# P transposed by row halves of the array into two PSUM banks, in one group with the next scores

## The chip, the core and the metric

The program runs on one core of a Trainium2 chip. The core has five engines that work side by side, each in the order of its own queue: TensorE (PE in the profile, with its weight loads as PEld), VectorE (DVE), ScalarE (ACT), GpSimd (POOL) and SyncE (SP), which issues transfers here. TensorE writes to PSUM, a memory of eight banks of 2 KB for each of 128 partitions; ScalarE and VectorE copy from there to SBUF. The metric is the device time of one execution in microseconds. All times below are in microseconds unless marked ns.

## What is computed

```python
# q, k, v: (8, 8, 576, 64) = (batch, heads, sequence, head size)
scores = scale * np.matmul(q, k.transpose(0, 1, 3, 2))
kth = np.partition(scores, -32, axis=-1)[..., -32:-31]
scores = np.where(scores >= kth, scores, -1e9)
attn = np.exp(scores - np.max(scores, axis=-1, keepdims=True))
attn = attn / (np.sum(attn, axis=-1, keepdims=True) + 1e-09)
x = np.matmul(attn, v)            # then (batch * sequence, heads * head size) = (4608, 512)
h = x @ w_in                      # (512, 2048)
g = 0.5 * h * (1.0 + erf(h / sqrt(2)))
out = g @ w_out                   # (2048, 512)
```

Attention that keeps the 32 largest scores of each row is followed by a two-layer perceptron with an exact gelu. Everything is 32-bit floating point on the chip; the two weight matrices arrive as 64-bit numbers and are converted there.

## The kernel before

**Items.** The attention is cut into 144 items. A main item is a pair of heads of one batch and 128 of the first 512 query rows; its tile `s` holds 2 x 576 scores for each of 128 rows. 576 keys are four blocks of 128 and a rest of 64, so the last 64 keys of both heads stand side by side in the middle of `s`. A last item (16 of 144, two per batch) takes the last 64 query rows of two pairs of heads.

**One item goes through the engines like this.** TensorE computes scores: `s_ps` for the 512 first keys (two banks, one for each head; each matmul uses 64 rows of the array, one half for each head) and `t_ps` for the last keys. ScalarE copies both to `s`. VectorE finds the 32nd largest of each row (`top_k`: four MAX8 and three MATCH_REPLACE8 for each head). GpSimd makes two small bias values of it (`threshold`). ScalarE runs `softmax` in two halves, one for each head: a Prelu that throws what is below the 32nd far down, and an Exp that also sums the row. GpSimd adds a small number to the sums (`add_small`, tile `den`), VectorE takes the reciprocal (`inverse`, tile `rden`) at the end of the next item's `top_k`, and GpSimd multiplies both heads' rows by it (`normalise`, in place in `s`). TensorE transposes the result P in blocks, ScalarE copies the transposed blocks to `pt` (or `ptt` for last items), and TensorE multiplies them with V (`attend`, tile `o`), for two main items at a time, so in every second iteration, and for each last item. ScalarE copies `o` to `xT`, from which the perceptron reads.

**The order is written out by hand.** The loop from line 659 emits every engine's queue. In iteration n it emits: scores of item n+2; attend of item n-3, if it completes a pair; the first half of softmax(n-1); up to eight pieces of the perceptron, spread between the others (`mlp`, 2 instructions of `y_ps` with 512 columns or 4 of `h_ps` with 256 columns each); the transposes of item n-2 in three pieces (the last keys' `tails`, then `main(0)` and `main(1)`, one for each head, each with its own copy); the second half of softmax(n-1) between `main(0)` and `main(1)`; `add_small(n-1)`; some transposes of later q and k (`prep`); gelus; and at the end top_k(n), inverse(n-1), threshold(n) and normalise(n-1). Up to iteration START = 10 both halves of the softmax come earlier, and `keep_busy` fills TensorE with idle matmuls. Pieces of the perceptron run once their tokens' `xT` is complete; what is left of them runs after the loop. The blocks of the perceptron alternate: eight `h` pieces in one iteration, eight `y` pieces in the next, with the two gelus of a block behind the `y` pieces. Gelu and Exp need different tables on ScalarE, so each alternation loads a table twice.

**PSUM.** `s_ps` has two banks and one buffer; the tag `tp` has two buffers of one bank, and takes turns through everything else of the attention: `t_ps`, the three transposes' tiles, `o`, and `tp_qk`. A tile that comes third waits until the first has been copied out. `h_ps` and `y_ps` have two banks each.

The places that the change and the prediction touch are `scores` (277), `softmax` (376 on), `transposes` (404), `attend` (452), and the loop (659).

Of the kernel before, what the change touches and what calls it, by code (L numbers as in the profile page):

```python
# [14 lines left out]
def kernel(  # L15
# [19 lines left out]
    nc = tc.nc  # L35
# [241 lines left out]
    def scores(i):  # L277
        if i >= N:
            return
# [3 lines left out]
        t_ps = ps.tile([P, 512], f32, tag="tp", name="t_ps")  # L283
        if t < NM:
            qk = qk_of[pair]
            lhsT = qk[:, t * P : (t + 1) * P]
            nc.tensor.matmul(t_ps[:, 0:P], lhsT=lhsT, rhs=qk[:, SM + P : KT], start=True, stop=True)  # L287
            for c in range(2):
                for e in range(2):
# [4 lines left out]
                    )  # L294
            if i == 0:
# [5 lines left out]
            nc.scalar.activation(spread(s, S + TL, SM), s_ps, func=AF.Copy, scale=scale)  # L301
            nc.scalar.activation(s[:, SM : S + TL], t_ps[:, 0:P], func=AF.Copy, scale=scale)
        else:
            for r in range(2):
# [9 lines left out]
            for r in range(2):  # L314
                qk = qk_of[pair + r]
                for e in range(2):
# [4 lines left out]
                    )  # L321
            s2 = s.rearrange("p (r n) -> p r n", r=2)
            nc.scalar.activation(s2[:, :, 0:SM], s_ps, func=AF.Copy, scale=scale)
            nc.scalar.activation(
# [78 lines left out]

    def transposes(i):

        if i < 0 or i >= N:
            return []
        t, s = items[i][1], S_of.pop(i)

        def tails():  # L410
            tp = ps.tile([P, 512], f32, tag="tp", name="tp_t")
            if t < NM:
                if t % 2 == 0:
                    pt_now[0] = work.tile([P, 2 * NM + 1, 2 * P], f32, tag="pt", name="pt")
                nc.tensor.transpose(tp[:, 0:P], s[:, SM : S + TL], ident)  # L415
                nc.scalar.copy(out=pt_now[0][:, 2 * NM, t % 2 * P : (t % 2 + 1) * P], in_=tp[:, 0:P])  # L416
            else:
                pt_now[0] = ptt
                for r in range(2):
                    nc.tensor.transpose(  # L420
                        tp[0:TL, r * P : (r + 1) * P], s[:, r * S + SM : (r + 1) * S], ident
                    )
                for e in range(2):
                    c = slice(e * TL, (e + 1) * TL)
                    nc.scalar.copy(
                        out=halves(ptt[c, 0, NM, :], e, NJ * P), in_=halves(tp[0:TL, 0 : 2 * P], e, P)
                    )

        def main(e):
            tp = ps.tile([P, 512], f32, tag="tp", name="tp")  # L430
            first = e * (S + TL if t < NM else S)
# [343 lines left out]
```

## Time and profile before

| | |
|---|---|
| time of three runs | 1637.06 median (1636.49 to 1637.59) |
| span of the profiled execution | 1634.7 |
| busy: TensorE, weight loads, VectorE, ScalarE, GpSimd | 1611.5, 1105.8, 1414.9, 1185.3, 665.3 |
| mean granted clock of TensorE | 0.999 |
| transposes of P, line 433 | 1152 matmuls of 128 x 128, 273 ns each |
| scores, line 291 | 1024 matmuls of 64 rows and 256 columns |
| copies of transposed P, line 440 | 256 + 32 of 512 columns, 575 ns |
| Exp, line 384 | 288, 776 ns; with 67 table loads of 1283 ns |
| normalise, line 396 | 278 of 1723 ns on GpSimd |

The profiled execution has no time of its own on record beside its span; its span lies 2.4 under the median of the runs, and 1.8 under the fastest. The table of busy time is an average over the whole; the loop's steady part, from about 205 to 1545, is what counts. A line of a timeline has the start, the length, the engine, the source line, the operation, the tile written and the tiles read, the shapes and how many instructions were merged. Matmuls overlap at their ends, so prices are read from start to start. A line of waits has the total, how often, and the longest.

### The profile page before, as it was taken

Reading aid. Unit: us, or ns where it says so; the run is one execution under the profiler, and the core shown is the slowest. Engines: PE = TensorE matmul, PEld = TensorE weight load, DVE = VectorE, ACT = ScalarE, POOL = GpSimd, SP = SyncE. Lnnn points to the kernel's source line nnn. Section 1 sums busy time; section 2 is a strip of 40 time slices with the busy share of each in tenths; the row PEclk is TensorE's granted clock in tenths of the full one; section 3 lists DMA queues with packets and bytes.
Section 4 is the critical chain, followed back from the end, with each engine's and each line's share of the span. In section 5 each row is a group of like instructions: output and inputs, shape, how many; then the busy total and the mean of one; then the engine's idle time right before and its main releaser. Section 6 shows DMA issues by size and latency. Waiting matters only on the chain.

```text
span 1634.7 us, 25758 instructions
## 1 busy us (share of the span) xinstructions
PE 1611.5 (99%) x9184; PEld 1105.8 (68%) x9184; DVE 1414.9 (87%) x3046; ACT 1185.3 (73%) x2132; POOL 665.3 (41%) x760
## 2 busy tenths in 40 slices
PE   7999999999999999999999999999999999999999
PEld 5776676766666666666666667676666666666665
DVE  8999999988898899998899899998889889999800
ACT  6989877777777777777777777777777777777720
POOL 4986833333333333333333333333333333333300
PEclk9999999999999999999999999999999999999999
DMA  6523210011101120001110111001110101000000
GB/s 165 157 76 117 81 43 1 14 40 33 36 1 28 30 58 1 14 19 33 29 28 15 28 30 43 1 14 36 37 36 1 28 16 36 1 14 4 4 14 13
DMA packets 126768, 56.19 MB, mean 34 GB/s; under 512 B 117776, under 2 KB 118064, under 8 KB 126640
## 3 DMA queue, kind: packets, MB, share of 16 engines
q1 hardware_dynamic: 125376, 54.12, 12.3%
q8 instruction: 73, 1.20, 0.3%
q10 hardware_dynamic: 1200, 0.39, 0.1%
q14 instruction: 55, 0.45, 0.1%
q0 software_dynamic: 64, 0.03, 0.0%
HBM read 45.08 MB, written 9.44 MB: 33 GB/s over the span
## 4 chain that ended last, share of the span: by engine, by line
PE 91%; DVE 5%; ACT 2%; POOL 1%; issue 0%; SPq 0%; DMA 0%; DVEq 0%; POOLq 0%; ACTq 0%
PE h_ps L522 30%; PE y_ps L558 30%; PE o L470 8%; PE s_ps L291 7%; PE tp L433 7%; DVE top L344 3%; DVE rest L347 2%; PE tp_qk L246 2%; PE t_ps L287 2%; PE o L481 1%; PE tp_t L415 1%; PE s_ps L318 1%; POOL s L396 1%; ACT s L384 0%; ACT s L383 0%
## 5 line engine op out<-in xcount | busy, mean ns | idle before, releaser
L344 DVE MAX8 top<-rest 128x8 f32<-128x576 f32 x864 | 610.0, 748 | 0.0
L522 PE MATMUL h_ps<-xT,w_in_sb 128*128 128x256 f32 (+1 forms) x2560 | 553.1, 361 | 0.0
L558 PE MATMUL y_ps<-w_out_sb,g 128*128 128x512 f32 x1152 | 548.9, 599 | 0.0
L396 POOL TENSOR_SCALAR s<-s,rden 128x576 f32<-128x576 f32 x278 | 476.5, 1723 | 0.6 <-DVE rden L370 0.4
L522 PEld LDWEIGHTS h_ps<-xT,w_in_sb 128*128 128x128 f32 x2560 | 428.4, 191 | 61.8 <-issue 16.4
L347 DVE MATCH_REPLACE8 rest<-top,rest 128x576 f32<-128x576 f32 x576 | 423.7, 744 | 0.0
L376 POOL TENSOR_SCALAR den<-den 128x2 f32<-128x2 f32 x144 | 32.0, 222 | 826.5 <-ACT s L384 826.0
L558 PEld LDWEIGHTS y_ps<-w_out_sb,g 128*128 128x128 f32 x1152 | 195.1, 190 | 168.2 <-issue 167.3
L301 ACT ACTIVATE s<-s_ps 128x1024 f32<-128x1024 f32 x127 | 130.6, 1028 | 164.9 <-PE s_ps L291 143.4
L384 ACT ACTIVATE s<-s,bias 128x576 f32<-128x576 f32 x288 | 223.4, 776 | 13.2 <-ACT s L383 0.7
L383 ACT ACTIVATE s<-s,neg 128x576 f32<-128x576 f32 x288 | 224.2, 778 | 0.3 <-POOL neg L359 0.2
L440 ACT COPY pt<-tp 128x512 f32<-128x512 f32 x256 | 146.8, 575 | 99.7 <-PE tp L433 99.6
L347 DVE MATCH_REPLACE8 rest<-top,s 128x576 f32<-128x576 f32 x288 | 211.9, 744 | 0.0
L433 PEld LDWEIGHTS tp<-ident,s 128*128 128x128 f32 x1152 | 142.5, 141 | 89.7 <-issue 58.9
L344 DVE MAX8 top<-s 128x8 f32<-128x576 f32 x288 | 201.9, 743 | 1.4 <-ACT s L297 1.4
L433 PE MATMUL tp<-ident,s 128*128 128x128 f32 x1152 | 172.7, 273 | 4.6 <-ACT pt L416 4.3
L470 PE MATMUL o<-pt,raw_v 128*64 128x256 f32 x1280 | 152.7, 385 | 0.5 <-ACT pt L440 0.5
L291 PE MATMUL s_ps<-qk 64*128 64x256 f32 x1024 | 146.1, 404 | 0.8 <-ACT s L299 0.8
L370 DVE RECIPROCAL rden<-den 128x2 f32<-128x2 f32 x144 | 23.2, 161 | 134.7 <-POOL den L376 134.4
L470 PEld LDWEIGHTS o<-pt,raw_v 128*64 128x64 f32 x1280 | 86.4, 137 | 64.4 <-issue 21.4
L533 ACT ACTIVATE g<-h_ps 128x512 f32<-128x512 f32 x144 | 78.6, 595 | 37.8 <-PE h_ps L522 37.1
L291 PEld LDWEIGHTS s_ps<-qk 64*128 64x128 f32 x1024 | 88.6, 187 | 22.2 <-ACT s L299 1.0
(77 smaller groups left out, 1155.7 us busy)
## 6 DMA issues: line engine op xcount, KB each, us to landing
raw_q<-in_q_dram SPq DMA_DIRECT2D x64, 128.0 KB, 2.4
raw_v<-in_v_dram SPq DMA_DIRECT2D x64, 128.0 KB, 2.5
raw_k<-in_k_dram SPq DMA_DIRECT2D x62, 128.0 KB, 2.5
out_dram<-y SPq DMA_DIRECT2D x31, 256.0 KB, 2.2
w_out_sb<-in_moe_w_in_dram SPq DMA_DIRECT2D x14, 511.8 KB, 5.1
w_out_sb<-in_moe_w_out_dram SPq DMA_DIRECT2D x10, 511.8 KB, 4.2
words<-in_moe_w_out_dram SPq DMA_DIRECT2D x6, 511.8 KB, 4.2
out_dram<-y SPq DMA_DIRECT2D x9, 128.0 KB, 2.3
```

Source lines behind the costliest of these rows:

```text
L291: nc.tensor.matmul(s_ps[:, e, c * 256 : (c + 1) * 256], lhsT=lhsT[rows, :], rhs=qk[rows, KT + c * 256 : KT + (c + 1) * 256], start=True, s ...
L301: nc.scalar.activation(spread(s, S + TL, SM), s_ps, func=AF.Copy, scale=scale)
L344: nc.vector.max(st["top"][:, e, 8 * r : 8 * r + 8], cur[e])
L347: nc.vector.match_replace(rest[:, e], st["top"][:, e, 8 * r : 8 * r + 8], cur[e], LOWEST)
L383: nc.scalar.activation(s, s, func=AF.Prelu, bias=st["neg"][:, e, 1:2], scale=1.0, alpha=STEEP)
L384: nc.scalar.activation(s, s, func=AF.Exp, bias=st["bias"][:, e : e + 1], scale=1.0, accum_out=st["den"][:, e : e + 1],)
L396: (nc.vector if e >= 2 - on_dve else nc.gpsimd).tensor_scalar(s, s, st["rden"][:, e : e + 1], None, op0=ALU.mult)
L433: nc.tensor.transpose(tp[:, j * P : (j + 1) * P], s[:, first + j * P : first + (j + 1) * P], ident)
L440: nc.scalar.copy(out=dst, in_=tp.rearrange("p (j n) -> p j n", j=NM))
L470: nc.tensor.matmul(o[e * D : (e + 1) * D, 0:n], lhsT=vt[:, j, e, :], rhs=pt[:, e * NM + j if j < NM else 2 * NM, :], start=(j == 0), stop= ...
L522: nc.tensor.matmul(h_tile(u)[:, i, :], lhsT=w_in_sb[:, ko, f * P : (f + 1) * P], rhs=xT[:, ko, c0 : c0 + n], start=(ko == 0), stop=(ko == ...
L558: nc.tensor.matmul(y_of[sub], lhsT=g_of[u][:, i, sub * P : (sub + 1) * P], rhs=w_out_sb[:, f, :], start=(f == 0), stop=(f == FT - 1),)
```

## The change

The three pieces of the transposes of item n-2 become one group that stands directly ahead of the scores of item n+2, and the group is moved within the iteration.

- Each 128 x 128 block is transposed as two halves of 64 rows. The halves alternate and write to two PSUM tiles, `tps[0]` and `tps[1]`, one for each half of the rows, so both heads' blocks of one row half share a bank. Sixteen small transposes take the place of eight; two copies of 512 columns stay two copies, with runs of 64 instead of 128.
- The transposes of the last keys (`tails`) write to the second quarter of `t_ps`, behind the scores of the last keys, and are copied between the copies of `s_ps` and of `t_ps`.
- In main items the last keys' scores come after the 512 first keys' instead of ahead. In last items `t_ps` still comes first.
- In the loop, attend(n-3) comes first, then (from iteration 11 on) one piece of the perceptron, or two in an iteration without attend, or none where the next piece's tokens are not ready; then the group of transposes and scores; then both halves of the softmax with pieces of the perceptron between.
- ScalarE's queue in an iteration then reads: two copies of transposed P, the score copy, the tail copy, the copy of the last keys' scores, Prelu and Exp of both heads, what is due of q/k copies, output copies and gelus, and the copy of the next attend.

```diff
-    def scores(i):
+    def scores(i, tails=None):
         if i >= N:
+            if tails:
+                t_ps = ps.tile([P, 512], f32, tag="tp", name="t_ps")
+                tails(t_ps)()
             return
...
         s_ps = ps.tile([P, 2, 512], f32, tag="s", bufs=1, name="s_ps")
-        t_ps = ps.tile([P, 512], f32, tag="tp", name="t_ps")
         if t < NM:
             qk = qk_of[pair]
             lhsT = qk[:, t * P : (t + 1) * P]
-            nc.tensor.matmul(t_ps[:, 0:P], lhsT=lhsT, rhs=qk[:, SM + P : KT], start=True, stop=True)
             for c in range(2):
...
+            t_ps = ps.tile([P, 512], f32, tag="tp", name="t_ps")
+            nc.tensor.matmul(t_ps[:, 0:P], lhsT=lhsT, rhs=qk[:, SM + P : KT], start=True, stop=True)
+            copy_tails = tails(t_ps) if tails else None
...
             nc.scalar.activation(spread(s, S + TL, SM), s_ps, func=AF.Copy, scale=scale)
+            if copy_tails:
+                copy_tails()
             nc.scalar.activation(s[:, SM : S + TL], t_ps[:, 0:P], func=AF.Copy, scale=scale)
         else:
+            t_ps = ps.tile([P, 512], f32, tag="tp", name="t_ps")
...
+            copy_tails = tails(t_ps) if tails else None
             s2 = s.rearrange("p (r n) -> p r n", r=2)
             nc.scalar.activation(s2[:, :, 0:SM], s_ps, func=AF.Copy, scale=scale)
+            if copy_tails:
+                copy_tails()
...
+    TC = 2 * TL
+
     def transposes(i):
...
+        first = [e * (S + TL if t < NM else S) for e in range(2)]
+        if t < NM and t % 2 == 0:
+            pt_now[0] = work.tile([P, 2 * NM + 1, 2 * P], f32, tag="pt", name="pt")
+        elif t == NM:
+            pt_now[0] = ptt
+        pt = pt_now[0]
+
+        tps = [ps.tile([P, 512], f32, tag="tp", name="tp") for _ in range(2)]
+        for e in range(2):
+            for j in range(NM):
+                at = (e * NM + j) * TL
+                for g in range(2):
+                    rows = slice(g * TL, (g + 1) * TL)
+                    nc.tensor.transpose(
+                        tps[g][:, at : at + TL],
+                        s[rows, first[e] + j * P : first[e] + (j + 1) * P], ident[rows, rows],
+                    )
+        for g in range(2):
             if t < NM:
+                c = t % 2 * P + g * TL
+                dst = pt[:, 0 : 2 * NM, c : c + TL]
+                src = tps[g].rearrange("p (j n) -> p j n", n=TL)
             else:
+                dst = pt[:, :, 0:NM, g * TL : (g + 1) * TL]
+                src = tps[g].rearrange("p (e j n) -> p e j n", e=2, n=TL)
+            nc.scalar.copy(out=dst, in_=src)
+
+        def tails(tp):
+
+            if t < NM:
+                nc.tensor.transpose(tp[:, TC : TC + P], s[:, SM : S + TL], ident)
+                return lambda: nc.scalar.copy(
+                    out=pt[:, 2 * NM, t % 2 * P : (t % 2 + 1) * P], in_=tp[:, TC : TC + P]
+                )
+            for r in range(2):
+                nc.tensor.transpose(
+                    tp[0:TL, TC + r * P : TC + (r + 1) * P], s[:, r * S + SM : (r + 1) * S], ident
+                )
...
+        return tails
...
-        scores(n + 2)
         product = attend(n - 3)
         late = n > START
-        if n <= START:
+        if not late:
 
             softmax(n - 1, 0)
         copy_x()
...
-        mlp(1)
-        tr = transposes(n - 2)
-        if product and n > START and done[0] < len(pieces) and pieces[done[0]][0] > ready[0]:
-
-            for piece in tr[:1]:
-                piece()
-            tr, ready[0] = tr[1:], n_tok[0]
-        if n > START:
+        if not (product and late and done[0] < len(pieces) and pieces[done[0]][0] > ready[0]):
+            mlp(1)
+            if not product:
+                mlp(1)
+        if n < START:
+
+            keep_busy((4 if product or n == 0 else 14) * (1 if n < 5 else 2), ident)
+
+        scores(n + 2, transposes(n - 2))
+        ready[0] = n_tok[0]
+        if late:
             softmax(n - 1, 0)
         mlp(1)
         if not late:
             softmax(n - 1, 1)
-        mlp(1)
-        if n < START:
-
-            keep_busy((4 if product or n == 0 else 14) * (1 if n < 5 else 2), ident)
...
-        for piece in tr[:-1]:
-            piece()
-            if n < START and product and piece is tr[0]:
-                keep_busy(5 if n < 5 else 10, ident)
-            ready[0] = n_tok[0]
-            mlp(1)
-        ready[0] = n_tok[0]
+        if n < START and product:
+            keep_busy(5 if n < 5 else 10, ident)
+        mlp(2)
         if late:
             softmax(n - 1, 1)
         add_small(n - 1)
...
-        for piece in tr[-1:] + prep:
+        for piece in prep:
             piece()
             mlp(1)
```

More of the change, by code (lines that the diff above doesn't have):

```diff
@@ L402 @@
     nc.gpsimd.memset(ptt[:, :, NM], 0.0)
+    TC = 2 * TL
     def transposes(i):
         if i < 0 or i >= N:
-            return []
+            return None
         t, s = items[i][1], S_of.pop(i)
-        def tails():
-            tp = ps.tile([P, 512], f32, tag="tp", name="tp_t")
+        first = [e * (S + TL if t < NM else S) for e in range(2)]
[15 more added lines that the diff above has]
+        for g in range(2):
@@ L412, in tails @@
             if t < NM:
[L413 to L416, printed above, removed]
-            else:
[L418 to L422, printed above, removed]
+                c = t % 2 * P + g * TL
@@ new lines, in transposes, with copy @@
+                dst = pt[:, 0 : 2 * NM, c : c + TL]
+                src = tps[g].rearrange("p (j n) -> p j n", n=TL)
+            else:
+                dst = pt[:, :, 0:NM, g * TL : (g + 1) * TL]
[11 more added lines that the diff above has]
+                )
+            def copy():
@@ L425, in tails @@
                     nc.scalar.copy(
-                        out=halves(ptt[c, 0, NM, :], e, NJ * P), in_=halves(tp[0:TL, 0 : 2 * P], e, P)
-                    )
-        def main(e):
-            tp = ps.tile([P, 512], f32, tag="tp", name="tp")
-            first = e * (S + TL if t < NM else S)
-            for j in range(NM):
-                nc.tensor.transpose(
-                    tp[:, j * P : (j + 1) * P], s[:, first + j * P : first + (j + 1) * P], ident
-                )
-            if t < NM:
-                dst = pt_now[0][:, e * NM : (e + 1) * NM, t % 2 * P : (t % 2 + 1) * P]
-            else:
-                dst = ptt[:, e, 0:NM, :]
-            nc.scalar.copy(out=dst, in_=tp.rearrange("p (j n) -> p j n", j=NM))
-        return [tails] + [lambda e=e: main(e) for e in range(2)]
+                        out=halves(pt[c, 0, NM, :], e, NJ * P),
+                        in_=halves(tp[0:TL, TC : TC + 2 * P], e, P),
+                    )
+            return copy
+        return tails
     def copy_x():
@@ L696 @@
             prep = []
-        if len(prep) > 1 and len(tr) == 3:
-            tr, prep = tr[:1] + prep[:1] + tr[1:], prep[1:]
-        for piece in tr[:-1]:
-            piece()
-            if n < START and product and piece is tr[0]:
-                keep_busy(5 if n < 5 else 10, ident)
-            ready[0] = n_tok[0]
-            mlp(1)
-        ready[0] = n_tok[0]
+        if n < START and product:
+            keep_busy(5 if n < 5 else 10, ident)
+        mlp(2)
         if late:
```

## The prediction

> **What bounds the kernel now.** I read the page's busy table and chain first, then the waits, then the timelines of TensorE, ScalarE and GpSimd over two neighbouring iterations.
>
> ```profile
> PE 1611.5 (99%) x9184; PEld 1105.8 (68%) x9184; DVE 1414.9 (87%) x3046; ACT 1185.3 (73%) x2132; POOL 665.3 (41%) x760
> PE 91%; DVE 5%; ACT 2%; POOL 1%; issue 0%; SPq 0%; DMA 0%; DVEq 0%; POOLq 0%; ACTq 0%
> ```
> TensorE (PE) is the bound. The waits say how far the others are ahead:
> ```profile
> DVE rden L370 <- POOL den L376: 134.4, 86, 8.7
> PE tp_t L415 <- POOL s L396: 3.5, 4, 1.4
> ```
> VectorE stands 134.4 us waiting for softmax sums; PE hardly ever waits (3.5 us) for the normalised P that it transposes. TensorE's timeline, start and length first:
> ```profile
> 594.83 1.39 PE L481 MATMUL o<-ptt,raw_v 128*64 128x64 f32 x40
> ...
> 800.85 0.33 PE L415 MATMUL tp_t<-ident,s 128*128 128x128 f32 x1
> ...
> 809.02 0.38 PE L287 MATMUL t_ps<-qk 128*128 128x128 f32 x2
> 809.33 1.13 PE L291 MATMUL s_ps<-qk 64*128 64x256 f32 x8
> 810.40 2.84 PE L558 MATMUL y_ps<-w_out_sb,g 128*128 128x512 f32 x6
> 813.08 0.27 PE L415 MATMUL tp_t<-ident,s 128*128 128x128 f32 x1
> ...
> 814.05 0.60 PE L433 MATMUL tp<-ident,s 128*128 128x128 f32 x4
> 814.48 1.02 PE L558 MATMUL y_ps<-w_out_sb,g 128*128 128x512 f32 x2
> ...
> 820.18 2.38 PE L470 MATMUL o<-pt,raw_v 128*64 128x256 f32 x20
> 822.49 2.86 PE L522 MATMUL h_ps<-xT,w_in_sb 128*128 128x256 f32 x12
> ...
> 830.49 0.39 PE L287 MATMUL t_ps<-qk 128*128 128x128 f32 x2
> 830.80 1.13 PE L291 MATMUL s_ps<-qk 64*128 64x256 f32 x8
> ```
> Starts give prices: a transpose 0.109 (814.05 to 814.48 for four), an MLP piece 0.86, scores 1.07, an attend 2.31, two iterations 21.47 (809.02 to 830.49). Over the trace, the reciprocals of items 18 and 140 start at 214.47 and 1528.70: 21.54 per two iterations. Then ScalarE and GpSimd:
> ```profile
> 822.87 0.78 ACT L383 ACTIVATE s<-s,neg 128x576 f32<-128x576 f32 x1
> 823.72 1.28 ACT L384 ACT_TABLE_LOAD   x1
> 825.02 0.78 ACT L384 ACTIVATE s<-s,bias 128x576 f32<-128x576 f32 x1
> ...
> 827.27 0.78 ACT L383 ACTIVATE s<-s,neg 128x576 f32<-128x576 f32 x1
> 828.08 0.77 ACT L384 ACTIVATE s<-s,bias 128x576 f32<-128x576 f32 x1
> ...
> 832.04 1.02 ACT L301 ACTIVATE s<-s_ps 128x1024 f32<-128x1024 f32 x1 [2.62 <-PE s_ps L291]
> 832.96 0.27 ACT L302 ACTIVATE s<-t_ps 128x128 f32<-128x128 f32 x1
> 833.12 0.78 ACT L383 ACTIVATE s<-s,neg 128x576 f32<-128x576 f32 x1
> ```
> ```profile
> 829.04 0.22 POOL L376 TENSOR_SCALAR den<-den 128x2 f32<-128x2 f32 x1 [7.88 <-ACT s L384]
> 829.83 3.42 POOL L396 TENSOR_SCALAR s<-s,rden 128x576 f32<-128x576 f32 x2
> ```
> Read here the path of one item: softmax on ScalarE (one Exp in two waits for a 1.28 us table load, after the gelus changed the table), then the sum, then 3.42 us of normalising on GpSimd. Today it ends about 2 us before PE asks for the result: here at 833.25.
>
> **PE's own work, part by part.**
> *Half-row transposes.* Eight transposes of 0.109 become sixteen of 64 rows by 64 columns, alternating halves. No row shows one. The nearest is L481, where two 64-column halves of the array alternate: 40 matmuls from 594.83, 594.83 + 1.39 - 0.22 for the last, is 0.058 a pair. Its loads are 64 columns wide, mine 128; but a transpose's load, where exposed, costs only the difference of 0.33 (800.85, just after a mode change) and 0.27: 0.06. So 0.058 a pair: 0.46 for 0.87. Ends: 0.055 (half a full transpose) and 0.109 (a full one); were the halves serial too, 0.218, a far end.
>
> The Trainium skill, "TensorE: Matmul & The Clock Gate", section "LDWEIGHTS (loading the stationary operand)", speaks against this edit: a load takes its columns over 1.2 per ns however few rows it has, 107 ns for 128. By it a pair would take 107 ns, nothing would be gained, and my sum would end near 1752. The exposed 0.06 disagrees with it, so I keep the row.
>
> *One group.* Scores also use 64-row halves, so transposes and scores share one change of mode each way. Per change the rows show about 0.10 of drain (1.07 for four pairs of 0.215 and one first load, leaves 0.10) and a first load of 0.10, or 0.06 for a transpose. The scores group goes from 0.31 + 1.07 + 0.10 + 9 x 0.109 = 2.46 to 0.16 (entry) + 0.51 (eight pairs, and the scores' first load) + 0.96 + 0.43 (last keys, tail transpose, first load) = 2.06.
> *Attend ahead.* It used to share the scores' change of mode; alone it pays 0.19 more. So -0.40 in an iteration without attend, -0.21 with: -0.61 of 21.47. Between items 18 and 140 run 61 such pairs: that alone would be -37 us.
> Warming matmuls, 1152 more small matmuls with their loads, and the V loads on SP that follow attend: taken at nothing, since the DVE floor (a reciprocal each 9.70 us) covers the first ten iterations and no PE wait of weight names a DMA; uncovered, 0 to 5 us. I put 2 us, with the ScalarE-heavy weight conversions, and below nothing only -2.
>
> **The wait that is added.** ScalarE runs in order. Before, the first half of softmax(n-1) stood ahead of the transposes' copies and the second behind one of them. After, both stand behind *two* tp copies, the score copy, the tail copy and the last-key copy, which all wait for PE's group; and the group's first instructions wait for GpSimd's normalise. That closes a ring once per iteration. Behind the waiting transposes stand scores, last keys, tail and all MLP pieces: PE stops.
>
> Ring, from T, the first transpose of the second head of item n-2, to the same of item n-1:
> - to the score copy's start: 0.17 (three pairs) + 0.10 + 0.64 (scores) + 0.38 (their length in L291's rows) + 0.11 (831.93 to 832.04) = 1.40; ScalarE's two tp copies, 0.48 each after 0.42, are done by then too (1.38);
> - score copy 0.92, tail 0.16, last keys 0.16: 2.64;
> - Prelu to Exp 0.87 (833.12 to 833.99 in ScalarE's timeline), Exp with its sum 0.77, second Prelu 0.81, Exp 0.68 to the sum, 0.28 to den, 0.79 to the normalise, 3.42: 7.62;
> - GpSimd's end to the transpose 0.05 to 0.11 (smallest gaps between those rows): 0.08.
> Sum 10.34; with the table load 1.28 more, 11.62.
>
> PE from T to T, no waiting: from an iteration without attend to one with: 0.27 + 0.96 + 0.43 + 6 x 0.86 + 0.24 (q/k transposes: 320 x 0.109 over 144) + attend 2.50 + 0.86 + 0.16 + 0.23 = 10.80. The other way, seven and two pieces and no attend: 10.03. Gelus follow the softmax in the iteration without attend, so the loaded Exp comes in the one with attend: its ring of 11.62 stands against 10.03. Two iterations: 10.80 + 11.62 = 22.42. Every fourth pair or so has y copies ahead of its gelus, and its first h piece finds PSUM 0.4 late: +0.10. Against 21.54 that is +0.98; 61 pairs: +60 us.
>
> **Last keys' scores (16 items).** In that branch t_ps is filled *before* s_ps. Both tp banks now hold P, so the t_ps matmul waits until ScalarE has copied the first: T + 0.17 + 0.22 + 0.03 + 0.56 + 0.07 = T + 1.05. Then 0.38 + 1.09 + 0.12 (t_ps, s_ps, wake; L307 and L318) put the score copy at 2.64 instead of 1.40: +1.24 in a loaded ring; in the other, 11.58 against 10.80: +0.78. Mean 1.01 x 16 = +16. Their tails take a second and longer copy, 0.35 in the loaded half: +3.
>
> **Sum:** 60 + 16 + 3 + 2 = +81. The profiled span of 1634.7 becomes 1715.7; the runs' median of 1637.06 lies 2.4 above the span, so 1718.
>
> **Rivals.**
> 1. *Half loads run at the full price* (the change doesn't do what it says): 0.051 more for each of 8 pairs on PE (10.80 to 11.21), 0.15 in the loaded ring: +0.56 a pair, 61 pairs, 1752. For it: L433's 0.109 with full loads; against: the 0.06.
> 2. *Faster: the normalised P is still ready in time.* Place: the wait at the group's first transposes. PE is then charged its own work: -37, + 16 x 0.68 for the last keys' bank: 1611. For it: the 3.5 us of such waits and the 2 us of slack now. Against: that slack came from MLP pieces between scores, tails and copies, and from the earlier first softmax half. It decides where the loaded ring falls from 11.62 to 10.03; break-even over pairs is 10.64 or so.
> 3. *Only the table load hides* (the Exp's table already loaded): 10.80 + 10.34 + 0.10 is -0.30 a pair, -18 + 16 + 3 + 2: 1640. Against: 67 such loads in the trace, each ahead of an Exp.
>
> **How the numbers follow.** Forecast 0.68 (1690 to 1742: each 0.3 us in the loaded ring is 18 us), rival 1 0.11, rival 2 0.12, rival 3 0.05, worse stalls 0.04. Range 1655 to 1757: it leaves out rivals 2 and 3 and little above. Within 0.2% (about what a measurement can tell here, 3.3 us) lies part of rival 3: 0.04. Faster 0.13, slower 0.83.
>
> **What would show it.** Sixteen tp matmuls in eight pairs 0.058 apart. PE waiting for the normalise, about 1.6 us in each second iteration, near 100 us in all, where 3.5 were; alternate iterations of about 10.8 and 11.6; VectorE's wait for den above 134 us; ScalarE's score copy 1.4 us after T, 2.6 for last keys. I am wrong if GpSimd's normalise ends before PE reaches the group in the iterations that follow a loaded Exp, or if the pairs stand 0.109 apart.

## The result, and the profile after

The changed kernel takes 1756.05 (median; 1753.92 to 1757.93), the kernel before 1637.32 beside it. The ratio is 1.0726, with a 95% interval of 1.0711 to 1.0741. It is slower, as forecast, and by 119 instead of 81.

The page of the changed kernel, its busy table and its chain:

```profile
PE 1618.2 (92%) x10336; PEld 1073.1 (61%) x10336; DVE 1419.1 (81%) x3046; ACT 1173.6 (67%) x2132; POOL 665.3 (38%) x760
...
PE 49%; ACT 30%; POOL 18%; issue 2%; DMA 1%; SPq 0%; POOLq 0%; ACTq 0%; DVE 0%; DVEq 0%
```

The chain that ended last was 91% TensorE before. Now a half of it goes through ScalarE and GpSimd: that is the ring of the prediction, from the group of transposes through the softmax and the normalise to the next group. The waits of the changed kernel (what waits, for whom, us in all, times, longest):

```profile
ACT pt L448 <- PE tp L436: 353.9, 128, 5.3
DVE rden L381 <- POOL den L387: 249.7, 140, 12.6
...
PE tp L436 <- POOL s L407: 95.5, 95, 4.2
...
PE t_ps L315 <- ACT pt L448: 10.6, 16, 0.7
```

TensorE waits 95.5 for the normalised P, where it waited 3.5. VectorE's wait for the sums went from 134.4 to 249.7. Of the 95.5, 68.2 lie between the reciprocals of items 18 and 140 and 24.8 in the first ten items. The last line is the bank of the last keys' scores, 0.66 in each of the 16 last items. The three timelines of one pair of iterations, TensorE's first (start, length, engine, line, operation; idle time before it and who ended it in brackets):

```profile
877.49 0.47 PE L436 MATMUL tp<-ident,s 64*128 64x64 f32 x8
878.47 0.46 PE L436 MATMUL tp<-ident,s 64*128 64x64 f32 x8 [0.51 <-POOL s L407]
878.77 1.08 PE L293 MATMUL s_ps<-qk 64*128 64x256 f32 x8
...
889.27 0.71 PE L436 MATMUL tp<-ident,s 64*128 64x64 f32 x16
889.82 0.43 PE L293 MATMUL s_ps<-qk 64*128 64x256 f32 x2
```

In the iteration without an attend, at 877.49, the first head's eight half transposes run, then TensorE stands until GpSimd has normalised the second head, with the scores and all that follows queued behind. ScalarE's timeline of the same stretch:

```profile
868.28 1.02 ACT L306 ACTIVATE s<-s_ps 128x1024 f32<-128x1024 f32 x1
...
870.38 1.28 ACT L395 ACT_TABLE_LOAD   x1
871.67 0.78 ACT L395 ACTIVATE s<-s,bias 128x576 f32<-128x576 f32 x1
...
873.24 0.78 ACT L395 ACTIVATE s<-s,bias 128x576 f32<-128x576 f32 x1
...
878.96 1.07 ACT L448 COPY pt<-tp 128x512 f32<-128x512 f32 x2 [4.60 <-PE tp L436]
```

And GpSimd's:

```profile
874.20 0.22 POOL L387 TENSOR_SCALAR den<-den 128x2 f32<-128x2 f32 x1 [7.60 <-ACT s L395]
...
874.99 3.43 POOL L407 TENSOR_SCALAR s<-s,rden 128x576 f32<-128x576 f32 x2
```

Read as one loop: score copy at 868.28, both softmax halves with the table load to 874.0, the sum at 874.20, the normalise to 878.42, the second head's transposes at 878.47. ScalarE, whose copies of P come next, stood idle for 4.60 in it.

A place without q/k transposes shows the length of two iterations, from the second head's first transpose to the next one (T of the prediction; in an unbroken group it stands 0.30 behind the first of the sixteen):

```profile
698.94 0.46 PE L436 MATMUL tp<-ident,s 64*128 64x64 f32 x8 [1.24 <-POOL s L407]
...
709.30 0.71 PE L436 MATMUL tp<-ident,s 64*128 64x64 f32 x16
...
721.23 0.46 PE L436 MATMUL tp<-ident,s 64*128 64x64 f32 x8 [1.24 <-POOL s L407]
```

From 698.94 to 709.60 it is 10.66, in which TensorE does not wait for P; from there to 721.23 it is 11.63, the ring with the table load. The second number comes back in nearly every pair of the steady stretch.

**Where the 120.4 went.** VectorE's reciprocals mark the items; the times are those from one marked reciprocal to the next.

| stretch | before | after | difference |
|---|---|---|---|
| to the reciprocal of item 0 | 29.5 | 29.6 | +0.1 |
| items 0 to 10 | 97.0 | 119.7 | +22.7 |
| items 10 to 18 | 88.0 | 96.0 | +8.1 |
| items 18 to 140 (61 pairs) | 1314.2 | 1398.0 | +83.7 |
| item 140 to the end | 106.0 | 111.8 | +5.8 |
| span | 1634.7 | 1755.2 | +120.4 |

The scores of the 16 last items fall four in items 10 to 18 and twelve in the steady stretch. So the forecast for the steady stretch was 60 for the ring and about 14 of the 19 for last keys and tails; it lost 83.7. The first ten items lost 22.7 where the forecast had 2. That stretch, as windows on the two kernels (the kernel before first; length, then busy time of PE, PEld, DVE, ACT and POOL, then the mean granted clock, the DMA share and GB/s):

```profile
0.00:126.52 126.52, 108.18 (x796) 87.36 (x797) 118.77 (x261) 105.85 (x174) 91.44 (x85) 0.99 0.48 139
```

The same of the changed kernel:

```profile
0.00:149.34 149.34, 115.31 (x880) 94.36 (x880) 119.78 (x261) 105.68 (x174) 91.30 (x85) 0.87 0.42 123
```

VectorE does the same 119 us of work, in 149 instead of 127: it isn't the floor there any more. And TensorE's granted clock fell from 0.99 to 0.87. GpSimd's timeline of the changed kernel in that stretch:

```profile
52.45 0.22 POOL L387 TENSOR_SCALAR den<-den 128x2 f32<-128x2 f32 x1 [3.27 <-ACT s L395]
52.75 2.42 POOL L210 TENSOR_TENSOR w_in_sb<-w_in_sb,words 128x1024 int32<-128x1024 int32 x1
...
55.63 3.43 POOL L407 TENSOR_SCALAR s<-s,rden 128x576 f32<-128x576 f32 x2
```

And TensorE's:

```profile
57.41 0.27 PE L436 MATMUL tp<-ident,s 64*128 64x64 f32 x1 [2.22 <-POOL s L407]
...
59.11 0.64 PE L436 MATMUL tp<-ident,s 64*128 64x64 f32 x8 [0.40 <-POOL s L407]
59.54 2.03 PE L293 MATMUL s_ps<-qk 64*128 64x256 f32 x8
```

The ring exists there too, and is longer: a part of the weights' conversion (2.42) stands in GpSimd's queue between the sum and the normalise, and the scores after the waits take 2.03 instead of 1.08. From 59.11: 2.50 to the score copy (61.61), 1.26 to the second Prelu (62.87), 1.77 to the sum (64.64), 0.30 to the weights' conversion (64.94), 2.43 for it, 0.5 for the bias, 3.43 for the normalise and 0.08: 12.27. Measured are 11.97 for each of the ten items on average, where VectorE's floor of 9.70 was taken to cover all. Without the 2.43 of conversion the same sum is 9.84, an estimate from these rows.

### The profile page after: what moved, and what is told of

It is laid out like the page before. It is cut to its first block, busy times and chain, and to the rows that moved or that the text cites. A ratio compares the mean times of both kernels' runs of the same rounds, so it can differ in the third digit from the quotient of the medians.

```text
span 1755.2 us, 28033 instructions
## 1 busy us (share of the span) xinstructions
PE 1618.2 (92%) x10336; PEld 1073.1 (61%) x10336; DVE 1419.1 (81%) x3046; ACT 1173.6 (67%) x2132; POOL 665.3 (38%) x760
## 3 DMA queue, kind: packets, MB, share of 16 engines
q8 instruction: 82, 1.34, 0.3%
## 4 chain that ended last, share of the span: by engine, by line
PE 49%; ACT 30%; POOL 18%; issue 2%; DMA 1%; SPq 0%; POOLq 0%; ACTq 0%; DVE 0%; DVEq 0%
PE y_ps L588 22%; POOL s L407 14%; ACT s L395 7%; PE o L500 7%; PE h_ps L552 6%; ACT s L394 6%; PE tp L436 5%; ACT L395 5%; ACT s L306 4%; ACT pt L448 4%; PE s_ps L293 4%; PE t_ps L298 1%; PE s_ps L326 1%; PE warm L666 1%; POOL neg L370 1%
## 5 line engine op out<-in xcount | busy, mean ns | idle before, releaser
L552 PE MATMUL h_ps<-xT,w_in_sb 128*128 128x256 f32 (+1 forms) x2560 | 535.0, 362 | 8.5 <-ACT g L563 8.5
L588 PE MATMUL y_ps<-w_out_sb,g 128*128 128x512 f32 x1152 | 528.7, 598 | 0.0
L552 PEld LDWEIGHTS h_ps<-xT,w_in_sb 128*128 128x128 f32 x2560 | 438.2, 191 | 73.8 <-issue 13.4
L448 ACT COPY pt<-tp 128x512 f32<-128x512 f32 x256 | 137.4, 589 | 353.9 <-PE tp L436 353.9
L588 PEld LDWEIGHTS y_ps<-w_out_sb,g 128*128 128x128 f32 x1152 | 212.9, 193 | 198.2 <-issue 194.8
L381 DVE RECIPROCAL rden<-den 128x2 f32<-128x2 f32 x144 | 23.8, 166 | 249.7 <-POOL den L387 249.7
L436 PE MATMUL tp<-ident,s 64*128 64x64 f32 x2304 | 128.0, 236 | 102.6 <-POOL s L407 95.5
L436 PEld LDWEIGHTS tp<-ident,s 64*128 64x128 f32 x2304 | 94.1, 141 | 192.8 <-POOL s L407 158.1
L293 PEld LDWEIGHTS s_ps<-qk 64*128 64x128 f32 x1024 | 92.4, 196 | 9.1 <-ACT s L304 1.0
```

Source lines behind the costliest of these rows:

```text
L293: nc.tensor.matmul(s_ps[:, e, c * 256 : (c + 1) * 256], lhsT=lhsT[rows, :], rhs=qk[rows, KT + c * 256 : KT + (c + 1) * 256], start=True, s ...
L436: nc.tensor.transpose(tps[g][:, at : at + TL], s[rows, first[e] + j * P : first[e] + (j + 1) * P], ident[rows, rows],)
L448: nc.scalar.copy(out=dst, in_=src)
L552: nc.tensor.matmul(h_tile(u)[:, i, :], lhsT=w_in_sb[:, ko, f * P : (f + 1) * P], rhs=xT[:, ko, c0 : c0 + n], start=(ko == 0), stop=(ko == ...
L588: nc.tensor.matmul(y_of[sub], lhsT=g_of[u][:, i, sub * P : (sub + 1) * P], rhs=w_out_sb[:, f, :], start=(f == 0), stop=(f == FT - 1),)
```

## The experiments

All are edits of the changed kernel but one (the kernel before with half rows). Each ratio is to the kernel before on the same chip. The stretches are those of the table above; a quiet pair is two iterations by the reciprocals, the median of the four pairs that begin at items 57 to 60, where no q/k transposes fall.

| kernel | time | ratio | items 0–10 | 10–18 | 18–140 | rest | quiet pair |
|---|---|---|---|---|---|---|---|
| before | 1637.3 | 1 | 97.0 | 88.0 | 1314.2 | 106.0 | 21.09 |
| after | 1756.1 | 1.0726 | 119.7 | 96.0 | 1398.0 | 111.8 | 22.30 |
| no table loads | 1667.7 | 1.0188 | 119.9 | 93.8 | 1316.4 | 108.2 | 21.03 |
| last keys after | 1733.2 | 1.0590 | 118.3 | 92.2 | 1379.6 | 110.1 | 22.30 |
| whole rows | 1784.0 | 1.0896 | 123.8 | 93.7 | 1426.0 | 108.6 | 23.02 |
| softmax first | 1844.1 | 1.1264 | 115.0 | 112.3 | 1466.2 | 116.3 | 20.27 |
| early softmax first | 1744.1 | 1.0659 | 111.7 | 95.8 | 1395.7 | 110.2 | 22.31 |
| normalise split | 1678.3 | 1.0252 | 118.4 | 95.4 | 1324.8 | 107.7 | 21.13 |
| copies late | 1679.0 | 1.0255 | 119.1 | 94.5 | 1324.2 | 110.8 | 21.05 |
| half rows in the old order | 1645.0 | 1.0045 | 105.2 | 89.8 | 1313.0 | 106.1 | 21.01 |
| x copy, then softmax first | 1973.3 | 1.2050 | 116.8 | 113.4 | 1586.4 | 123.7 | 25.01 |
| three mends | 1646.0 | 1.0059 | 98.7 | 91.5 | 1314.5 | 107.7 | 21.13 |
| four mends | 1640.1 | 1.0021 | 99.1 | 93.6 | 1308.2 | 107.7 | 20.68 |
| four mends, half the split | 1652.9 | 1.0100 | 100.3 | 92.1 | 1316.0 | 110.9 | 20.89 |

### Without the table loads

```diff
-            nc.scalar.activation(g_of[u], h_of.pop(u), func=AF.Gelu)
+            nc.scalar.activation(g_of[u], h_of.pop(u), func=AF.Prelu, alpha=0.1)
```

> The gelus are replaced by a Prelu of the same size, which needs no other table than Exp, so the 68 + 67 table loads go; the output is not the reference's. Theory: the loaded ring loses 1.28 and becomes the unloaded one of 10.40, PE's 10.8 binds in the other iteration; two iterations go from 22.92 to about 21.5, 61 pairs: about 1670 (1655 to 1690). Rival (half-row transposes on PE are slow): table loads are not on the path, 1745 or more.

1667.73, a ratio of 1.0188 (1.0173 to 1.0203). The steady stretch fell by 81.6, which is 1.34 a pair for a table load of 1.28. The loads ahead of the gelus went as well, but they stand behind the softmax, off the ring. So the table load lies on the ring in full, once in two iterations; from T to T they now take 10.35 and 10.66 in quiet places. The first ten items, in which no gelu runs, kept their 119.9.

### The last keys' scores after the first keys'

```diff
         else:
+            for r in range(2):
+                qk = qk_of[pair + r]
+                for e in range(2):
+                    rows = slice(e * D, (e + 1) * D)
+                    nc.tensor.matmul(
+                        s_ps[half(r, e), r, :], lhsT=qk[rows, SM + e * TL : SM + (e + 1) * TL],
+                        rhs=qk[rows, KT:], start=True, stop=True,
+                    )
             t_ps = ps.tile([P, 512], f32, tag="tp", name="t_ps")
...
-            for r in range(2):
...
             copy_tails = tails(t_ps) if tails else None
```

> In the 16 last items the scores of the last keys come after those of the 512 first keys, as in main items. Theory: takes back the +16 of the wait for the first tp bank (0.9 to 1.2 in each of 16): 1736 to 1744. Rival (that wait lies in the shadow of another): no change within 3.

1733.22, 1.0590 (1.0575 to 1.0606): 22.8 less (12 to 20 had been expected), 1.43 on average for each of the 16 last items, where 1.01 had been charged. The difference is in TensorE's speed in six of them. The timeline of a last item of the changed kernel:

```profile
600.97 0.46 PE L436 MATMUL tp<-ident,s 64*128 64x64 f32 x8 [1.24 <-POOL s L407]
602.10 0.70 PE L315 MATMUL t_ps<-qk 128*64 128x64 f32 x8 [0.67 <-ACT pt L448]
602.73 1.99 PE L326 MATMUL s_ps<-qk 64*64 64x512 f32 x8
...
616.39 1.09 PE L326 MATMUL s_ps<-qk 64*64 64x512 f32 x8
```

After waits of 1.24 and 0.67 these scores take 1.99, and 1.09 in the next last item, where only the 0.67 stands before them. The longest single matmul of line 326 took 1113 ns in the changed kernel, 640 in the kernel before and 642 here. Eight of the 16 last items have both waits; in six of these the scores' longest matmul took 712 to 1113 ns, and the mean granted clock over the 4 us behind the first wait was 0.62 to 0.79. These six took 2.1 to 2.3 longer than here from group to group, seven of the other ten 1.1. The bank's wait was a true cost; that it also brought a slower TensorE was not in the sum.

### Whole rows in the group

```diff
             for j in range(NM):
-                at = (e * NM + j) * TL
-                for g in range(2):
-                    rows = slice(g * TL, (g + 1) * TL)
-                    nc.tensor.transpose(
-                        tps[g][:, at : at + TL],
-                        s[rows, first[e] + j * P : first[e] + (j + 1) * P], ident[rows, rows],
-                    )
-        for g in range(2):
+                nc.tensor.transpose(
+                    tps[e][:, j * P : (j + 1) * P],
+                    s[:, first[e] + j * P : first[e] + (j + 1) * P], ident,
+                )
+        for e in range(2):
...
```

> The group stays where it is, with its two copies ahead of the scores' copy, but the transposes are eight of 128 rows again (one head for each bank). Theory: PE is not what binds in the loaded iteration, so taking the half rows back gains nothing; the ring grows by about 0.15 (four transposes of 0.109 for four pairs of 0.058) and a change of mode of 0.10, PE's side by 0.5: about 1775 (1762 to 1795). Rival (half rows are what slows): 1700 or less. Second rival (half rows gain nothing, a pair costs as much as a full transpose): within 5 of 1756.

1783.95, 1.0896 (1.0878 to 1.0914). The steady pair went from 22.92 to 23.38. So within the group the half rows are worth 0.46 a pair, 28 us in all, on the ring as it is: this part of the change does what it says. One group of eight whole transposes in TensorE's timeline of this kernel:

```profile
881.83 1.31 PE L433 MATMUL tp<-ident,s 128*128 128x128 f32 x8
```

The sixteen halves shown above run from 889.27 to the scores at 889.82; less 0.10 for the scores' first load, that is 0.056 a pair.

### Both softmax halves ahead of the group

```diff
-        if not late:
-            softmax(n - 1, 0)
+        softmax(n - 1, 0)
+        if late:
+            softmax(n - 1, 1)
         copy_x()
...
         scores(n + 2, transposes(n - 2))
-        if late:
-            softmax(n - 1, 0)
...
-        if late:
-            softmax(n - 1, 1)
```

> Both halves of softmax(n-1) are put ahead of the group of transposes and scores in every iteration from 11 on; nothing else differs from the changed kernel. Theory (a ring of transposes, ScalarE copies, softmax, GpSimd normalise and the next transposes sets the period): the ring then spans two iterations and PE's own work binds, two iterations go from 22.92 to about 21, so about 1650 (1625 to 1690, since softmax now stands behind output copies and gelus in ScalarE's queue and may come late in some iterations). PE's wait for the normalise falls from 95.5 to under 30, what is left being in the first ten iterations. Rival (the small half-row transposes, their changes of mode or the order on PE cost the time): no less than 1735.

1844.06, 1.1264 (1.1247 to 1.1281): the other way. The waits of this kernel:

```profile
ACT qk L250 <- PE tp_qk L246: 180.1, 86, 4.3
...
PE tp L436 <- ACT xT L505: 101.6, 45, 4.9
...
PE tp L436 <- POOL s L407: 23.9, 15, 4.2
```

The wait for the normalise is gone (the 23.9 lie in the early items). In the quiet place TensorE does not wait at all:

```profile
726.88 0.71 PE L436 MATMUL tp<-ident,s 64*128 64x64 f32 x16
...
736.73 0.71 PE L436 MATMUL tp<-ident,s 64*128 64x64 f32 x16
...
747.34 0.72 PE L436 MATMUL tp<-ident,s 64*128 64x64 f32 x16
```

So TensorE's own work there is 9.85 and 10.61 for the two iterations, 20.46, and 20.50 for the next two (767.84), where the kernel before has 21.03 and 21.26 between its scores in such a place (636.47, 657.50, 678.76). But attend's tile `o` takes one of the two `tp` banks, and its copy to `xT` now stands behind the softmax: TensorE waits 101.6 for that bank, and ScalarE then 180.1 for the q/k transposes that TensorE has not reached. My expectation had followed one ring and not the other tiles that turn through the same two banks.

### The same, with the copy of x first

```diff
+        copy_x()
         softmax(n - 1, 0)
         if late:
             softmax(n - 1, 1)
-        copy_x()
```

> As the kernel with both softmax halves ahead of the group (1844, a miss), but the copy of attend's result comes ahead of the softmax too. Reading of that miss: the softmax stood between attend and that copy, the copy frees one of the two tp banks, and PE waited 101.6 for it; so this wait should fall under 15 and the time by about 100, to 1740 (1690 to 1790; ScalarE still waits 180 for q/k transposes that stand ahead of the softmax). Rival (the miss has to do with the softmax being too early for VectorE's results): the time stays above 1815.

1973.31, 1.2050 (1.2032 to 1.2068), a second miss. The wait for `xT` went (4.3), and a larger one came: 143.0 of the last keys' scores for the copies to `pt`. TensorE's timeline of this kernel:

```profile
918.31 0.71 PE L436 MATMUL tp<-ident,s 64*128 64x64 f32 x16
...
922.76 0.49 PE L298 MATMUL t_ps<-qk 128*128 128x128 f32 x2 [2.82 <-ACT pt L448]
```

And ScalarE's:

```profile
918.51 1.28 ACT L395 ACT_TABLE_LOAD   x1
...
922.14 1.05 ACT L448 COPY pt<-tp 128x512 f32<-128x512 f32 x2
```

P's transposes are done by 919, but their copies stand behind the softmax until 922.14, and the last keys' scores need the bank. With two banks, whichever copy stands behind the softmax is waited for.

### Softmax first in the early items alone

```diff
             softmax(n - 1, 0)
+            softmax(n - 1, 1)
         copy_x()
...
-        if not late:
-            softmax(n - 1, 1)
```

> Up to iteration 10 both halves of softmax(n-1) come ahead of the group, as in the kernel before; later iterations stay as changed. Items 0 to 10 took 119.7 from reciprocal to reciprocal after the change and 97.0 before. Theory (the same ring, here with the weight conversions of 2.42 on GpSimd in it, held the first stage): 97 to 103 again and a time of 1732 to 1742. Rival (the moved idle matmuls and the clock of 0.87 that came with them are the cause by themselves): the stage stays above 112.

1744.14, 1.0659 (1.0639 to 1.0680). Items 1 to 5 went back to 9.70 each; then the copy of x behind the softmax held the bank, as TensorE's timeline of this kernel shows, and the stretch ended at 111.7, a gain of 8.1, with a miss on its size (97 to 103 was expected):

```profile
77.82 0.67 PE L436 MATMUL tp<-ident,s 64*128 64x64 f32 x14 [3.43 <-ACT xT L505]
```

With the copy of x ahead of the softmax (in the kernels with three and four mends below) the same stretch took 98.7 and 99.1, against 97.0 before. In these kernels the idle matmuls stay where the change put them. So the place of the second softmax half and of the copy of x in ScalarE's queue was the cause of the early loss; the copy of x ahead by itself wasn't tried.

### The second head's normalise on VectorE

```diff
-        normalise(n - 1, 2 if on_pool(u) else 0)
+        normalise(n - 1, 2 if on_pool(u) else 1 if n > START else 0)
```

(The number is how many heads VectorE normalises.)

> From iteration 11 on the second head's normalise goes to VectorE, which stands waiting 249.7 in the changed kernel; GpSimd keeps the first head. Theory: the ring loses one normalise of 1.72 less the first head's four pairs, to about 8.9 and 10.2 with the table load, and PE's own 10.8 and 10.0 bind; two iterations go from 22.92 to about 21.2, so 1650 (1635 to 1668). Rival (copies and bank waits on PE's side bind, not the normalise): above 1730; VectorE becoming the bound by its extra half microsecond for each item would show as a reciprocal period of 10.3 and as no wait for den.

1678.34, 1.0252 (1.0236 to 1.0267). The ring lost one of its two 1.72 on GpSimd: the steady pair fell from 22.92 to 21.72, and TensorE's wait for the normalise from 95.5 to 43.2, of which 19.4 lie in the steady stretch. It is less than expected (1635 to 1668), and the time lies outside. VectorE now needs 10.36 for an item, but it is not the bound of the quiet pair: it still waits 55.6 for the sums in the steady stretch. The groups on TensorE start 10.61 apart, which is its own work, and 10.50, which is still the ring with the table load:

```profile
690.13 0.22 POOL L387 TENSOR_SCALAR den<-den 128x2 f32<-128x2 f32 x1 [7.97 <-ACT s L395]
...
690.75 0.49 POOL L373 TENSOR_TENSOR bias<-neg 128x2 f32<-128x2 f32 x1
691.22 1.72 POOL L407 TENSOR_SCALAR s<-s,rden 128x576 f32<-128x576 f32 x1
```

GpSimd's queue has the bias of the next item ahead of the normalise, and where VectorE normalises beside it the bias took 0.49, for 0.19 in the changed kernel: 0.30 of what was expected of the ring. Why it is slower there was not tested.

### The score copies behind the softmax

```diff
-        scores(n + 2, transposes(n - 2))
+        copies_out = scores(n + 2, transposes(n - 2))
+        if not late:
+            copies_out()
...
             softmax(n - 1, 1)
+            copies_out()
```

> From iteration 11 on ScalarE's copies of the scores, the tail and the last keys' scores come behind both halves of the softmax; the copies of transposed P stay ahead. Theory: the ring loses 0.92 + 0.16 + 0.16 = 1.24, so 9.1 and 10.4, PE binds in the unloaded one; two iterations about 21.3, 1660 (1645 to 1690, since t_ps's bank and the s_ps banks are held about 3 longer and q/k transposes may wait for them). Rival (the softmax merely comes late because PE's group is late, ring not closed): no change within 10.

1678.95, 1.0255 (1.0240 to 1.0270). The copies of scores, tails and last keys (1.24 together) no longer stand between the group and the softmax. The steady pair fell by 1.21, to 21.71, and the loaded ring in quiet places is 10.37 from T to T, where 11.63 less 1.24 is 10.39.

### Half rows in the old order

The kernel before, whose `main(0)` now transposes both heads in half rows; the two copies stay where they were.

```diff
-            tp = ps.tile([P, 512], f32, tag="tp", name="tp")
...
+            if e == 0:
+                tps.extend(ps.tile([P, 512], f32, tag="tp", name="tp") for _ in range(2))
+                for e in range(2):
+                    for j in range(NM):
+                        at = (e * NM + j) * TL
+                        for g in range(2):
+                            rows = slice(g * TL, (g + 1) * TL)
+                            nc.tensor.transpose(
+                                tps[g][:, at : at + TL],
+                                s[rows, first[e] + j * P : first[e] + (j + 1) * P], ident[rows, rows],
+                            )
```

> The kernel before with the half-row transposes alone, in the place of main(0); loop, softmax and scores as before. Theory: halves save 0.41 in each iteration and pay their own change of mode both ways, 0.16 and 0.20, and ring and slack stay as they were: 1637 within 15. Rival (a half-row pair costs as much as a full transpose, or half rows disturb PE by themselves): 1690 or more.

1645.01, 1.0045 (1.0029 to 1.0062). The steady stretch is the one of before (1313.0 against 1314.2), though the sixteen halves take 0.65 from start to start here (0.87 for eight whole ones). The half rows alone cost nothing there and bring nothing; 8.1 of the 9.2 by which its span grew are in the first ten items, where the granted clock fell to 0.92. TensorE's timeline shows where the 0.22 of a group goes:

```profile
651.12 1.02 PE L574 MATMUL y_ps<-w_out_sb,g 128*128 128x512 f32 x2
652.08 0.71 PE L441 MATMUL tp<-ident,s 64*128 64x64 f32 x16
652.72 3.70 PE L574 MATMUL y_ps<-w_out_sb,g 128*128 128x512 f32 x8
656.26 0.38 PE L287 MATMUL t_ps<-qk 128*128 128x128 f32 x2
```

At 0.43 for each matmul of `y_ps`, two and eight of them take 0.86 and 3.44; here it is 0.96 to the group and 3.54 behind it. So 0.10 is lost on each side, where matmuls of 128 rows and of 64 meet, and the group costs 0.84 for 0.87. By the profile the group's weight loads wait 60.7 in all for the copy of the tails, which sets the second bank free, but that isn't the cost: TensorE itself waits 1.4 in the steady stretch, and in the softmax-first kernel the group starts as late behind its `y_ps` (1.81 for four, 734.92 to 736.73) without such a wait. In the changed kernel the scores share these changes.

### Three mends, four mends, and half of one

The normalise split and the last keys after, as above, and in the early items the copy of x and the whole softmax ahead of the group:

```diff
+        copy_x()
         if not late:
 
             softmax(n - 1, 0)
-        copy_x()
+            softmax(n - 1, 1)
```

> Second head normalised on VectorE, last keys' scores after the first keys', and up to iteration 10 attend's copy and then both softmax halves ahead of the group. Theory: 1678 less 18 (last keys, as in that run's steady part) less 15 to 20 (first stage back to about 100): 1642 (1630 to 1656). Rival (the three remove the same wait): no better than 1665.

1645.99, 1.0059 (1.0042 to 1.0076), as expected: 110 of the 119 are back. With the late copies as well:

> All of the former, and the score copies behind the softmax. Theory: both cuts of the ring together (1.5 and 1.24) leave PE alone as the bound in the steady part: two iterations about 20.9 (PE's own 20.85), against 21.54 in the kernel before, a span of 1600 to 1625, 1615. That is faster than the kernel before if the half rows in the shared group really save PE's 0.61 for two iterations. Rival (half rows save PE nothing): two iterations at 21.4 or more, 1640 or more. A third end: VectorE, with half a microsecond more for each item and 9.72 for its own work, binds with reciprocals 10.3 apart.

1640.08, 1.0021 (1.0012 to 1.0031), a miss: 1600 to 1625 was expected. VectorE's timeline of this kernel, in a quiet place:

```profile
664.13 0.14 DVE L389 RECIPROCAL rden<-den 128x2 f32<-128x2 f32 x1
664.38 0.52 DVE L415 TENSOR_SCALAR s<-s,rden 128x576 f32<-128x576 f32 x1
...
674.47 0.15 DVE L389 RECIPROCAL rden<-den 128x2 f32<-128x2 f32 x1
```

VectorE does not wait here, and its reciprocals are 10.34 apart: 20.68 for a quiet pair, more than the 20.46 that TensorE takes from group to group. Over the whole steady stretch TensorE binds again: it is busy 1289.3 of 1308.2, 21.1 a pair, and VectorE waits 41.8 there. The expectation had 20.9 a pair for TensorE. Why its saving is 0.57 or more in a quiet pair and 0.4 over all pairs stays open. The steady stretch is 6.0 better than before the change; items 10 to 18 give 5.6 of it back, the early items 2.1 and the rest 1.7. Last, with the split only in iterations with an attend:

```diff
-        normalise(n - 1, 2 if on_pool(u) else 1 if n > START else 0)
+        normalise(n - 1, 2 if on_pool(u) else 1 if n > START and product else 0)
```

> The kernel of the run before it (the second head's normalise on VectorE, the last keys' scores behind the first keys', early copies of x and softmax ahead of the group, and from iteration 11 the score copies behind both softmax halves), but VectorE takes the second head's normalise only in iterations with an attend, where the Exp table is loaded. Theory: in that run VectorE's half microsecond in every iteration was the bound (reciprocals 10.34 apart in quiet places, 20.68 for two); taken only where the ring is long, two iterations of VectorE are 9.70 + 10.34 = 20.04, TensorE alone binds again, with about 20.5 in quiet places and 0.43 more for the q/k transposes where they fall, and the 61 pairs gain some 0.2 to 0.4 each: 1628 (1618 to 1640), a little below the kernel before. Rival: GpSimd, which now normalises two heads (3.43) in the unloaded iterations, closes the unloaded ring at about 10.4 ahead of TensorE's 10.03 to 10.8, and the early iterations, where its weight additions stand, get longer again: 1641 to 1655, no better than the run before.

1652.87, 1.0100 (1.0083 to 1.0116), a miss. VectorE's timeline of this kernel:

```profile
656.06 0.15 DVE L389 RECIPROCAL rden<-den 128x2 f32<-128x2 f32 x1
...
666.59 0.17 DVE L389 RECIPROCAL rden<-den 128x2 f32<-128x2 f32 x1 [0.74 <-POOL den L395]
666.86 0.52 DVE L415 TENSOR_SCALAR s<-s,rden 128x576 f32<-128x576 f32 x1
...
676.95 0.15 DVE L389 RECIPROCAL rden<-den 128x2 f32<-128x2 f32 x1
```

The split was put on the wrong item. The long iteration runs from one item's normalise, through the group, to the loaded softmax of the next. That first normalise now had both heads on GpSimd (3.43, from 656.71), so the loaded softmax was late, and VectorE waited 0.74 for its sum. The split came after it, ahead of the unloaded softmax, which had 2.05 to spare (its sum at 674.90, the reciprocal at 676.95). Two iterations take 10.53 + 10.36. The rival's time (1641 to 1655) holds, but not by its reason, the unloaded ring. The split in the other iterations wasn't tried. No version beat the kernel before.

## Why the prediction was right or wrong

**The ring, right.** The wait that the change adds closes where it was said, at its length: from T to T 11.63 with the table load, for a forecast of 11.62, and 10.35 where the loads were taken away, for 10.34. The other iteration takes 10.66 in a quiet place, TensorE's own work, for a forecast of 10.80 less 0.24 of q/k transposes. Each of three terms, taken away by itself, shortened the steady pair: the table load by 1.34, the score copies by 1.21, a head of the normalise by 1.20. The steady 61 pairs lost 83.7 for about 74; 6 of the rest are the last keys (18.4 in that stretch when undone, for 12). The sign "near 100" for TensorE's wait came out at 95.5 in part by luck: 68.2 of it are in the steady stretch, 1.1 a pair, and 24.8 in the early items, for which no such wait had been put.

**PE's own work, right in size and off the path.** The pairs of half rows stand 0.056 apart (forecast 0.058), not 0.109. A quiet pair in which TensorE never waits took 20.46 (softmax first); the steps gave 10.80 + 10.03, less 0.48 for the q/k transposes, 20.35. That is 0.57 less than before (0.76 in the next pair), for a forecast of 0.61. But TensorE waited, so none of the 37 us came through in the changed kernel, and in the old order half rows gained nothing, since the two sides of each group took back what the halves saved.

**The last keys, mechanism right, term too small.** 22.8 when undone, where 16 stood, since in six of the 16 items the granted clock fell to 0.62 to 0.79 behind the waits.

**The step that failed: the early stage "taken at nothing, since the DVE floor (a reciprocal each 9.70 us) covers the first ten iterations".** It lost 22.7, where 2 had been put. (Items 10 to 18 lost another 8.1; four last items fall there, and 3.8 came back with the last keys after.) The floor covers work on TensorE that is shorter than it. It doesn't cover a ring that goes through VectorE's own input: there the second softmax half moved behind the copies as well, the ring held 2.42 of weight conversion on GpSimd, and at 12.27 it was longer than the floor. I had named what stands behind each wait for the steady iterations, and had not done so for these. A slower granted clock (0.87) added to it: the scores in that ring took 2.03 for 1.08. The forecast time was 1718; that the measured one still lies in the range, 1 us below its end of 1757, is luck, since the range was made for the steady ring.

**The end.** +5.8 where nothing was put. From the reciprocal of item 140 to that of 143 it is 33.3 against 28.6, and 29.3 without the table loads, so the ring goes on there. But it is 31.6 in two kernels whose edits lie elsewhere; how much of the 5.8 is the ring was not separated.

**The rivals.** Rival 1 (1752) is near the time by accident: its pairs of 0.109 aren't there. The Trainium skill, "TensorE: Matmul & The Clock Gate", section "LDWEIGHTS (loading the stationary operand)", puts a load at its columns over 1.2 per ns whatever its rows, which makes 107 ns for 128 columns, an estimate; no run here shows that price for these halves, and the measured 56 ns a pair decides. Rival 2 (1611) fell with the wait of 95.5. The slack that spoke for it was smaller than read: in the kernel before the normalise ends at 833.25, and the first transpose that needs it, the tails', starts at 834.54. Rival 3 (1640) fell with the table load's 81.6.

## What to carry to other kernels

When an edit moves work in an in-order queue, follow the ring for every stage of the loop, also for stages that another engine's floor seems to cover: a floor hides only what doesn't feed it. With two buffers in turn, list all tiles that use them and where each one's copy stands in its queue; here three reorderings of ScalarE's queue moved the wait to the next tile. An engine's saving is worth nothing until the loop it waits in is shorter than its own work.

## What was not expected of the hardware

TensorE's granted clock was lower behind some waits, short ones among them. In the first 149 us it was 0.87 on average, with waits of up to 4.2 for the normalise; eight score matmuls took 2.03 after waits of 2.22, 0.57 and 0.40 in a row, and the clock from 59.10 to 62.30 was 0.52. In the steady stretch, where the longest wait for the normalise was 1.24, the mean was 0.99: behind waits of 0.30 and 1.24 at 698.94 the scores took 1.08 at a clock of 1.00. A last item's 1.24 and 0.67 slowed its scores to 1.99 (clock 0.62 from 600.97 to 604.90), but the same two waits at 1014.56 left the clock at 1.00, and of the eight items with both waits two kept it. In the old order with half rows, the first ten items had 0.92, with waits of up to 1.6. The Trainium skill, "TensorE: Matmul & The Clock Gate", section "What's actually happening", has two speeds, half and full, set by how busy the array was in a free-running window of about 3.4 us; score matmuls of nearly double length (2.03 for 1.08), and equal waits with unequal clocks, fit that, and no run here shows the window itself.
